# Chunked linear attention feeding a bilinear FFN: the inter-block products in 64x64 tiles of the array

## The chip, the core and the metric

The kernel runs on one core of a Trainium2 chip. The metric is device time in microseconds, the median over several executions. The core has a matrix engine (TensorE, "PE" in the profile, with its weight loads shown as "PEld"), a vector engine (VectorE, "DVE"), an activation engine (ScalarE, "ACT"), GpSimdE ("POOL"), and a queue of DMA issues on SyncE ("SP"). Matrix products are written to PSUM, a memory in banks. DVE and ACT carry results from PSUM to SBUF.

## What is computed

`q`, `k`, `v` are `[4, 8, 768, 64]` (batch, heads, sequence, head width), `lam` is one decay for each head. The reference walks over blocks of the sequence:

```python
intra = einsum('bhic,bhjc->bhij', qb, kb) * Dmask        # lam**(i-j) for i >= j, else 0
intra = einsum('bhij,bhjd->bhid', intra, vb)
inter = einsum('bhid,bhde->bhie', qb * lam_pow, kv_state) # what earlier blocks left
out   = intra + inter
kv_state = lam_block * kv_state + einsum('bhsd,bhse->bhde', kb_dec, vb)
...
x = out as [3072, 512]                                    # heads side by side
result = ((x @ w_a) * (x @ w_b)) @ w_out                  # w_a, w_b: 512x1536, w_out: 1536x512
```

## The kernel before

**Units.** The sequence is cut into blocks of 128 rows. A unit is one block of one batch with all 8 heads, so there are 4 x 6 = 24 units (`NB` = 6 for each batch), and unit `u` follows unit `u-1` in its batch unless `u % NB == 0`. The decay is folded into the operands: `make_qs` and `make_ks` multiply q by `lam**pos` and k by `lam**-pos` (POOL, L272 and L277), so that the state is a plain running sum, and the mask is plain lower-triangular.

**One unit's attention.** Its q and k are turned to `qT`, `kT` with heads in pairs: pair `hp` holds heads `2hp` and `2hp+1` in partitions 0-63 and 64-127. `scores` (L323) makes 8 products, K = 64 rows of the array each, the two heads of a pair in two PSUM banks. `masks` (L340, DVE) makes bf16 copies of both banks under the triangle. `intra` (L365) makes 8 products with `vb`, each 64 columns wide, into one PSUM bank `o_ps` `[128, 4, 128]`. `inter` (L355) adds 4 products of 128x128: the state of a pair is kept as a 128x128 matrix with the two heads' 64x64 states on its diagonal and zeros elsewhere. `evac_o` (L372) copies the bank to `xT`, the input of the FFN.

**The state.** `kv_mms` (L379) accumulates `k^T v` of a unit in the PSUM bank `kvd`, 4 products of 128x128 (whole pairs, so that the off-diagonal blocks hold products of different heads). `kv_copy` (L411, DVE) multiplies 128x512 of it by a mask `bdiag` of ones on the diagonal blocks, into `st_bufs`. Where a pair of units has just gone through `pieces_O`, `kv_beside` (L400) adds the second unit's state with 8 products of 64 columns instead.

**The FFN.** Units are taken in groups of `GROUPS = (4, 1, 2, 4, 4, 4, 4, 1)`. For a group, each of 12 column chunks `f` gives 4 products for `a_ps`, 4 for `b_ps` (both L449), an ACT copy to `a_sb` (L457) and a DVE product `ab` (L462); then 12 products for each unit make `op` (L482), ACT copies it (L477) and SP stores it.

**Order.** The schedule is manual: the program's order is each engine's order. `ffn` calls `hook(slot)` after each chunk, and the table `PLAN` says which attention pieces of later units are put there: `P` (load, scale and transposition by DMA), `V` (`kv_update` and `kv_copy`), `S` (`scores`, `masks`), `O`/`O2` (`pieces_O` for one or two units) and `Q` (`pieces_O` for two units, with the scores of the next two in between). PSUM banks are handed out in rotation, 7 of them, by `ps_bank`; the eighth holds `kvd`.

**Start.** The first four units go another way: q and k arrive packed (`x4`), are scaled by `scale4` on DVE (L553), transposed on PE (`transpose4`), scored (`scores4`), and their state and outputs are made before the FFN begins. All loads stand in one queue in the order q, k, v, then the weights in chunks of 512 KB (`w_a` chunk 0, 1, `w_b` chunk 0, 1, ...); `cast_w` turns each chunk to bf16. `cast_w("a", 0, "first")` (L171 to L173) splits the first chunk between DVE and POOL. In the first group chunk `f = 0` is made in two column cuts, units 0-2 and then unit 3.

Of the kernel before, what the change touches and what calls it, by code (L numbers as in the profile page):

```python
# [66 lines left out]
def kernel(  # L67
# [94 lines left out]
    def cast_w(kind, c, eng):  # L162
        t = staged.pop((kind, c))
        if kind == "o":
            dst = wo_sb[:, 2 * c:2 * c + 2, :]
        else:
            dst = w_part(wa_sb if kind == "a" else wb_sb, c)
        if eng == "act":
            nc.scalar.copy(dst, t)  # L169
        elif eng == "first":  # L170
            nc.vector.tensor_copy(dst[:, :2, :128], t[:, :2, :128])  # L171
            nc.gpsimd.tensor_copy(dst[:, 2:, :128], t[:, 2:, :128])
            nc.gpsimd.tensor_copy(dst[:, :, 128:], t[:, :, 128:])  # L173
        else:
            nc.vector.tensor_copy(dst, t)  # L175
        pump()
# [39 lines left out]
    for w, src in (("q", q), ("k", k)):  # L216
        x4_r = src[0, :, 0:PACK * BLK, :].rearrange("h (p r) d -> p h (r d)", r=PACK)
        n_h = 4 if w == "q" else 2
        for h in range(0, H, n_h):
            t = wst_pool.tile([128, 1024], F32, name=w + "4", tag="wst")[:, :n_h * 256]  # L220
            nc.sync.dma_start(out=t.rearrange("p (h x) -> p h x", h=n_h), in_=x4_r[:, h:h + n_h])
            t = t.rearrange("p (h r d) -> p h r d", h=n_h, r=PACK)
            for hh in range(0, n_h, 2):
                x4[w, h + hh] = t[:, hh:hh + 2]
            staged[w + "4", h] = t
# [20 lines left out]
    bdiag = singles.tile([128, 2, 64], BF16, name="bdiag")  # L246
    nc.gpsimd.memset(bdiag, 0.0)
    nc.gpsimd.memset(bdiag[0:64, 0, :], 1.0)
    nc.gpsimd.memset(bdiag[64:128, 1, :], 1.0)
    st_bufs = [singles.tile([128, HP, 2, D], BF16, name=f"st{i}") for i in range(4)]  # L250
    for t in st_bufs:
        nc.gpsimd.memset(t, 0.0)
# [8 lines left out]
    bdiag_bc = _bc(bdiag, [bdiag.ap[0], [0, HP], [1, 128]])  # L261
# [7 lines left out]

    def make_ks(u, eng):  # L270
        qk = prep_pool.tile([128, 2, H, D], BF16, name="qk", tag="qk")
        eng_of(eng).tensor_mul(qk[:, 1], raw.pop((u, "k")),  # L272
                               lp_k[:, u % NB].to_broadcast([128, H, D]))
        U[u] = dict(qk=qk, kn=qk[:, 1])

    def make_qs(u, eng):
        eng_of(eng).tensor_mul(U[u]["qk"][:, 0], raw.pop((u, "q")),  # L277
                               lp_q[:, u % NB].to_broadcast([128, H, D]))
# [65 lines left out]
    def o_bank(u):  # L344
        first = "o" not in U[u]
        if first:
            U[u]["o"] = ps_bank("o_ps", [128, HP, 128], F32)
        return first

    def inter(u):  # L350
        d = U[u]
        if u % NB > 0:
            first = o_bank(u)
            for hp in range(HP):
                nc.tensor.matmul(d["o"][:, hp, :], lhsT=st_bufs[(u - 1) % 4][:, hp, :, :],  # L355
                                 rhs=d["qT"][:, hp, :], start=(first and hp == 0), stop=True,
                                 skip_group_check=True)

    def intra(u, first=False):
        d = U[u]  # L360
        first = o_bank(u) or first
        for hp in range(HP):
            for i in range(2):
                p = slice(64 * i, 64 * i + 64)
                nc.tensor.matmul(d["o"][p, hp, :], lhsT=d["vb"][:, 2 * hp + i, :],  # L365
                                 rhs=d["m"](i, hp), start=(first and hp == 0),
                                 stop=True, skip_group_check=True)

    def evac_o(u, xT, col, eng="act"):
        o_ps = U[u].pop("o")  # L370
        if eng == "act":
            nc.scalar.copy(xT[:, :, col:col + BLK], o_ps)  # L372
        else:
            nc.vector.tensor_copy(xT[:, :, col:col + BLK], o_ps)

    def kv_mms(ps, w, hps, first):
        d = U[w]
        for hp in hps:
            nc.tensor.matmul(ps[:, hp, :, :], lhsT=d["kn"][:, 2 * hp:2 * hp + 2, :],  # L379
                             rhs=d["vb"][:, 2 * hp:2 * hp + 2, :], start=(first and hp == 0),  # L380
                             stop=True, skip_group_check=True)

    def kv_bank():
        kv["ps"] = kvps_pool.tile([128, HP, 2, D], F32, name="kvd", tag="kvd")
# [9 lines left out]
    def kv_beside(u):  # L394
        if u % NB == 0 or u % NB == NB - 1:
            kv_update(u)
        for hp in range(HP if 0 < u % NB < NB - 1 else 0):
            for i in range(2):
                p = slice(64 * i, 64 * i + 64)
                nc.tensor.matmul(kv["ps"][p, hp, i, :], lhsT=U[u]["kn"][:, 2 * hp + i, :],  # L400
                                 rhs=U[u]["vb"][:, 2 * hp + i, :],
                                 start=False, stop=True, skip_group_check=True)

    def kv_copy(u, ps, eng="dve"):
        st = st_bufs[u % 4]
        if eng == "act":
            for i in range(2):
                p = slice(64 * i, 64 * i + 64)
                nc.scalar.copy(st[p, :, i, :], ps[p, :, i, :])
        else:  # L410
            nc.vector.tensor_mul(st[:].rearrange("p hp i d -> p hp (i d)"),  # L411
                                 ps[:].rearrange("p hp i d -> p hp (i d)"), bdiag_bc)
# [11 lines left out]
    def pieces_O(us, nxt=()):  # L424
        kqs = [score_banks() for u in nxt]
        for u in us:
# [3 lines left out]
        for u in us:  # L430
            intra(u)
            xT, col = xTs[u]
            evac_o(u, xT, col)
        if len(us) == 2 and us[0] >= n0 + 5:
            kv_beside(us[1])
        for u, kq in zip(nxt, kqs):
            masks(u, kq)
        if len(us) == 2 and us[0] >= n0 + 5 and us[1] % NB < NB - 1:
# [6 lines left out]
    def half(w_sb, f, xT, gt, name, cuts=None):  # L445
        ps = ps_bank(name, [128, 512], F32, ffn=True)
        for lo, hi in cuts or ((0, gt),):
            for s in range(KS):
                nc.tensor.matmul(ps[:, lo:hi], lhsT=w_sb[:, s, f * 128:(f + 1) * 128],  # L449
                                 rhs=xT[:, s, lo:hi], start=(s == 0), stop=(s == KS - 1),  # L450
                                 skip_group_check=bool(cuts))
        return ps

    def a_part(f, xT, gt, cuts=None):
        ps = half(wa_sb, f, xT, gt, "a_ps", cuts)
# [3 lines left out]

    def b_part(f, xT, gt, a_sb, ab):  # L460
        ps = half(wb_sb, f, xT, gt, "b_ps")
# [23 lines left out]
    def ffn(u0, n, xT, hook, first, last):  # L485
        gt = n * BLK
        ab = ab_pool.tile([128, FC, 512], BF16, name="ab", tag="ab")
        if first:
            for i, cs in enumerate(W_STEPS):
                nxt = W_STEPS[i + 1] if i + 1 < len(W_STEPS) else ()  # L490
                fs = range(w_off[cs[0]] // 128, w_off[cs[-1] + 1] // 128)
                a_sbs = [a_part(f, xT, gt, ((0, gt - BLK), (gt - BLK, gt)) if f == 0 else None)
                         for f in fs]
# [57 lines left out]
    def scale4(w, i, j):  # L551
        hs = slice(4 * i + 2 * j, 4 * i + 2 * j + 2)
        nc.vector.tensor_mul(  # L553
            xs4[w].rearrange("p r (h d) -> p h r d", d=D)[:, hs],
            x4[w, hs.start],
            (lp_q if w == "q" else lp_k)[:, NB:, hs, :].rearrange("p r h o -> p h r o")
            .to_broadcast([128, 2, PACK, D]))
        if w == "k" or j == 1:
            staged.pop((w + "4", 4 * i + (2 * j if w == "k" else 0)))
# [173 lines left out]
```

## Time and profile before

| | |
|---|---|
| median of 5 runs | 232.93 us (232.57 to 233.85) |
| the profiled execution's own time | 232.71 us |
| its span in the profile | 231.0 us, so 1.71 us lie around it |
| PE busy | 225.1 us (97%), 1763 products |
| DVE, ACT, POOL busy | 117.1, 88.7, 50.8 us |
| granted TensorE clock | 1.0 |
| DMA | 39.36 MB, mean 170 GB/s |

A line of the timeline has its start and its length in us, the engine, the line of the kernel, the operation, output and inputs, shapes, how many instructions were merged, and in brackets the idle time before it with what ended it. The length of a merged row of products includes the way of the last one through the array; so the time that a group of products takes from PE is read as the start of the next group less its own start. `128*64` in a PE row says how many rows and columns of the array each product uses; the shape after it is rows by streamed columns.

### The profile page before, as it was taken

How to read it: one execution, taken by the hardware profiler on the slowest of the kernel's cores; microseconds unless marked ns; L12 is line 12 of the kernel's file. 1: busy time of each engine (PE TensorE's matmuls, PEld its weight loads, DVE VectorE, ACT ScalarE, POOL GpSimd, SP SyncE). 2: the span in 40 equal slices, each digit the busy share in tenths (PEclk: the TensorE clock that was granted, in tenths of full speed). 3: DMA queues.
4: the chain of work that ended last, by engine and by line, in shares of the span. 5: the costliest groups of instructions: out<-in, count | busy, mean ns of one | idle time of the engine just before them, and what ended most of it. 6: DMA issues, size and time to landing. Idle time of an engine off the chain costs nothing.

```text
span 231.0 us, 4496 instructions
## 1 busy us (share of the span) xinstructions
PE 225.1 (97%) x1763; PEld 124.1 (54%) x1763; DVE 117.1 (51%) x205; ACT 88.7 (38%) x170; POOL 50.8 (22%) x65
## 2 busy tenths in 40 slices
PE   7899999999999999999999999999999999999994
PEld 2575444459687554554544454544454544444493
DVE  0894856636569738675324583325583313332050
ACT  3577553066442243342233342233332234332261
POOL 6061000238351444433301533002100000000000
PEclk9999999999999999999999999999999999999999
DMA  4999999999999999999969996239200220000311
GB/s 149 305 279 350 364 386 270 306 218 193 207 207 175 219 193 210 224 184 232 356 207 204 215 186 100 91 115 207 45 3 0 91 91 3 1 0 18 121 45 48
DMA packets 97509, 39.36 MB, mean 170 GB/s; under 512 B 85456, under 2 KB 91984, under 8 KB 97488
## 3 DMA queue, kind: packets, MB, share of 16 engines
q1 hardware_dynamic: 97200, 39.00, 74.4%
q8 instruction: 14, 0.23, 0.4%
q10 hardware_dynamic: 288, 0.07, 0.1%
q14 instruction: 7, 0.06, 0.1%
HBM read 28.32 MB, written 6.29 MB: 150 GB/s over the span
## 4 chain that ended last, share of the span: by engine, by line
PE 91%; DMA 3%; DVE 3%; ACT 1%; issue 1%; SPq 0%; DVEq 0%
PE a_ps L449 27%; PE op L482 27%; PE b_ps L449 26%; PE o_ps L365 3%; DMA q<-in_q_dram 3%; PE kq L323 2%; PE o_ps L355 2%; PE kvd L379 1%; ACT scratch L576 1%; DVE m L340 1%; DVE ab L462 1%; PE tps L309 1%; DVE scratch L553 1%; PE kq L601 1%; DVE st L411 0%
## 5 line engine op out<-in xcount | busy, mean ns | idle before, releaser
L462 DVE TENSOR_TENSOR ab<-a_sb,b_ps 128x512 bf16<-128x512 bf16 (+2 forms) x96 | 52.2, 552 | 76.7 <-PE b_ps L449 57.8
L449 PE MATMUL a_ps<-xT,wa_sb 128*128 128x512 bf16 (+3 forms) x388 | 76.9, 324 | 0.2 <-ACT xT L372 0.2
L449 PE MATMUL b_ps<-xT,wb_sb 128*128 128x512 bf16 (+2 forms) x384 | 76.9, 326 | 0.0
L457 ACT CAST a_sb<-a_ps 128x512 bf16<-128x512 f32 (+2 forms) x96 | 45.2, 480 | 62.3 <-PE a_ps L449 62.2
L482 PE MATMUL op<-wo_sb,ab 128*128 128x512 bf16 (+2 forms) x312 | 65.6, 363 | 0.0
L449 PEld LDWEIGHTS <-wb_sb 128*128 128x128 bf16 x384 | 34.5, 98 | 28.6 <-ACT wb_sb L169 0.2
L449 PEld LDWEIGHTS <-wa_sb 128*128 128x128 bf16 x388 | 34.0, 98 | 28.6 <-DVE wa_sb L175 0.8
L482 PEld LDWEIGHTS <-ab 128*128 128x128 bf16 x312 | 28.7, 98 | 30.0
L340 DVE TENSOR_TENSOR m<-kq,lotri 128x512 bf16<-128x512 f32 x47 | 29.3, 683 | 18.3 <-PE kq L323 17.7
L272 POOL TENSOR_TENSOR qk<-kf,lp_k 128x512 bf16<-128x512 f32 x18 | 19.0, 1053 | 73.7 <-DMA kf<-in_k_dram 58.4
L277 POOL TENSOR_TENSOR qk<-qf,lp_q 128x512 bf16<-128x512 f32 x20 | 22.0, 1101 | 22.5 <-DMA qf<-in_q_dram 22.5
L477 ACT COPY o_sb<-op 128x512 f32<-128x512 f32 (+2 forms) x19 | 10.3, 540 | 34.0 <-PE op L482 34.0
L372 ACT CAST xT<-o_ps 128x512 bf16<-128x512 f32 x22 | 12.0, 588 | 18.5 <-PE o_ps L365 17.9
L411 DVE TENSOR_TENSOR st<-kvd,bdiag 128x512 bf16<-128x512 f32 x18 | 12.3, 683 | 3.4 <-PE kvd L379 3.4
L286 DVE CAST vb<-vf 128x512 bf16<-128x512 f32 x17 | 10.8, 636 | 1.7 <-DMA vf<-in_v_dram 1.3
L208 PE MATMUL idle<-idle_sb 128*128 128x128 bf16 (+1 forms) x31 | 7.7, 392 | 1.3 <-DVE idle_sb L203 1.3
L365 PE MATMUL o_ps<-m,vb 128*64 128x128 bf16 x192 | 7.8, 222 | 0.0
L286 POOL CAST vb<-vf 128x512 bf16<-128x512 f32 x7 | 4.8, 679 | 13.8 <-DMA vf<-in_v_dram 13.8
L355 PEld LDWEIGHTS <-st 128*128 128x128 bf16 x80 | 5.4, 98 | 3.2 <-issue 0.4
L311 ACT COPY qkT<-tps 128x1024 bf16<-128x1024 bf16 x3 | 3.0, 1012 | 10.4 <-PE tps L309 10.4
L323 PE MATMUL kq<-qkT 64*128 64x128 bf16 x160 | 6.7, 218 | 0.0
L169 ACT CAST wb_sb<-wst 128x1024 bf16<-128x1024 f32 x5 | 5.2, 1046 | 3.3 <-DMA wst<-in_moe_w_b_dram 3.3
(58 smaller groups left out, 85.7 us busy)
## 6 DMA issues: line engine op xcount, KB each, us to landing
vf<-in_v_dram SPq DMA_DIRECT2D x24, 256.0 KB, 4.9
qf<-in_q_dram SPq DMA_DIRECT2D x20, 256.0 KB, 4.3
kf<-in_k_dram SPq DMA_DIRECT2D x20, 256.0 KB, 4.8
out_dram<-o_sb SPq DMA_DIRECT2D x16, 256.0 KB, 2.0
wst<-in_moe_w_a_dram SPq DMA_DIRECT2D x6, 512.0 KB, 8.6
wst<-in_moe_w_b_dram SPq DMA_DIRECT2D x6, 512.0 KB, 9.1
wst<-in_moe_w_out_dram SPq DMA_DIRECT2D x6, 512.0 KB, 10.7
out_dram<-o_kept SPq DMA_DIRECT2D x7, 256.0 KB, 3.4
```

The costliest lines, as they stand in the source:

```text
L272: eng_of(eng).tensor_mul(qk[:, 1], raw.pop((u, "k")), lp_k[:, u % NB].to_broadcast([128, H, D]))
L277: eng_of(eng).tensor_mul(U[u]["qk"][:, 0], raw.pop((u, "q")), lp_q[:, u % NB].to_broadcast([128, H, D]))
L286: eng_of(eng).tensor_copy(vb, vf)
L323: nc.tensor.matmul(kq[i][:, hp, :], lhsT=d["kT"][p, hp, :], rhs=d["qT"][p, hp, :], start=True, stop=True, skip_group_check=True)
L340: nc.vector.tensor_mul(m, kq[i], lotri_bc)
L365: nc.tensor.matmul(d["o"][p, hp, :], lhsT=d["vb"][:, 2 * hp + i, :], rhs=d["m"](i, hp), start=(first and hp == 0), stop=True, skip_group_c ...
L372: nc.scalar.copy(xT[:, :, col:col + BLK], o_ps)
L411: nc.vector.tensor_mul(st[:].rearrange("p hp i d -> p hp (i d)"), ps[:].rearrange("p hp i d -> p hp (i d)"), bdiag_bc)
L449: nc.tensor.matmul(ps[:, lo:hi], lhsT=w_sb[:, s, f * 128:(f + 1) * 128], rhs=xT[:, s, lo:hi], start=(s == 0), stop=(s == KS - 1), skip_gro ...
L457: nc.scalar.copy(a_sb[:, :gt], ps[:, :gt])
L462: nc.vector.tensor_mul(ab[:, f, :gt], a_sb[:, :gt], ps[:, :gt])
L482: nc.tensor.matmul(op[:, lo:hi], lhsT=ab[:, f, t * 128:(t + 1) * 128], rhs=wo_sb[:, f, lo:hi], start=(f == 0), stop=(f == FC - 1))
```

## The change

1. Heads are paired 4 apart: pair `c` holds heads `c` and `c+4`. `scale` writes q and k in that order with a pattern of four dimensions, and the packed loads of the start bring heads `c` and `c+4` (4 loads of q instead of 2, of half the size).
2. `inter` makes 8 products of 64 rows and 64 columns of the array for a unit, in the order of the four quarters, instead of 4 of 128x128.
3. `kv_mms` makes 8 products of 64 columns (streaming 64) for every update instead of 4 of 128x128; `kv_beside` goes. The state is kept without zero blocks: `kv_copy` is a plain copy of 128x256, `bdiag` and the clearing of `st_bufs` go.
4. A pair of units shares two `o_ps` banks, one for heads 0-3 and one for heads 4-7 (the row halves of the array that write them), and `evac_o` copies a bank for both units at once. A single unit takes two banks and two smaller copies.
5. At the start, the first two chunks `f` are made in two column halves (units 0, 1, then 2, 3: `a_parts`), DVE casts three quarters of the first weight columns instead of a half, and intra and inter products of units 0 to 3 stand in a new order.

The core of the diff:

```diff
-            nc.vector.tensor_copy(dst[:, :2, :128], t[:, :2, :128])
-            nc.gpsimd.tensor_copy(dst[:, 2:, :128], t[:, 2:, :128])
+            nc.vector.tensor_copy(dst[:, :3, :128], t[:, :3, :128])
+            nc.gpsimd.tensor_copy(dst[:, 3:, :128], t[:, 3:, :128])
...
-        n_h = 4 if w == "q" else 2
-        for h in range(0, H, n_h):
-            t = wst_pool.tile([128, 1024], F32, name=w + "4", tag="wst")[:, :n_h * 256]
-            nc.sync.dma_start(out=t.rearrange("p (h x) -> p h x", h=n_h), in_=x4_r[:, h:h + n_h])
...
+        x4_r = x4_r.rearrange("p (b c) x -> p c b x", b=2)
+        n_c = 2 if w == "q" else 1
+        for c in range(0, HP, n_c):
+            t = wst_pool.tile([128, 1024], F32, name=w + "4", tag="wst")[:, :n_c * 512]
+            t = t.rearrange("p (c b x) -> p c b x", c=n_c, b=2)
+            for cc in range(n_c):
+                nc.sync.dma_start(out=t[:, cc], in_=x4_r[:, c + cc])
...
-    st_bufs = [singles.tile([128, HP, 2, D], BF16, name=f"st{i}") for i in range(4)]
-    for t in st_bufs:
-        nc.gpsimd.memset(t, 0.0)
+    st_bufs = [singles.tile([128, HP, D], BF16, name=f"st{i}") for i in range(4)]
...
+    def scale(eng, dst, x, lp):
+        eng_of(eng).tensor_mul(dst.rearrange("p (c b) d -> p b c d", b=2),
+                               x[:].rearrange("p (b c) d -> p b c d", b=2),
+                               lp.rearrange("p (b c) o -> p b c o", b=2)
+                               .to_broadcast([128, 2, HP, D]))
...
+    def o_banks(us, ats=(None, None)):
+        for b, at in enumerate(ats):
+            ps = ps_bank("o_ps", [128, 2, 2, BLK], F32, at=at)
+            for n, u in enumerate(us):
+                U[u].setdefault("o", []).append(ps[:, :, n, :])
...
+    def o_mm(u, b, c, **ops):
+        h = 4 * b + c
+        p = slice(64 * (h % 2), 64 * (h % 2) + 64)
+        new = U[u]["flags"]
+        nc.tensor.matmul(U[u]["o"][b][p, c // 2, :], start=new[b, h % 2], stop=True,
+                         skip_group_check=True, **ops)
...
     def inter(u):
...
-                nc.tensor.matmul(d["o"][:, hp, :], lhsT=st_bufs[(u - 1) % 4][:, hp, :, :],
-                                 rhs=d["qT"][:, hp, :], start=(first and hp == 0), stop=True,
-                                 skip_group_check=True)
+            for c in range(HP):
+                for b in range(2):
+                    p = slice(64 * b, 64 * b + 64)
+                    o_mm(u, b, c, lhsT=st[p, c, :], rhs=U[u]["qT"][p, c, :])
...
+    def intra(u, b):
+        for c in range(HP):
+            o_mm(u, b, c, lhsT=U[u]["vb"][:, 4 * b + c, :], rhs=U[u]["m"](b, c))
...
+    def kv_mms(ps, w, cs, first):
+        d = U[w]
+        for c in cs:
+            for b in range(2):
+                nc.tensor.matmul(ps[64 * b:64 * b + 64, c, :], lhsT=d["kn"][:, 2 * c + b, :],
+                                 rhs=d["vb"][:, 4 * b + c, :], start=(first and c == 0),
                                  stop=True, skip_group_check=True)
...
-            nc.vector.tensor_mul(st[:].rearrange("p hp i d -> p hp (i d)"),
-                                 ps[:].rearrange("p hp i d -> p hp (i d)"), bdiag_bc)
+            nc.vector.tensor_copy(st, ps)
...
+        for b in range(2):
+            for u in us:
+                intra(u, b)
+            evac_o(us, b)
...
+    def a_parts(fs, xT, gt):
+        ps_parts[0] = True
+        pss = [half(wa_sb, f, xT, "a_ps", 0, gt // 2) for f in fs]
+        a_sbs = []
+        for f, ps in zip(fs, pss):
+            half(wa_sb, f, xT, "a_ps", gt // 2, gt, ps)
+            a_sbs.append(a_copy(ps, gt))
```

## Prediction

> **What bounds the kernel now.** I read the busy time by stage first, then PE's own timeline, then what PE waited for. By stage:
>
> ```profile
> core 0: us, PE busy (x) PEld busy (x) DVE busy (x) ACT busy (x) POOL busy (x), PEclk, DMA share, GB/s
> 5.00:20.00 15.00, 13.94 (x184) 9.36 (x183) 12.27 (x20) 10.06 (x20) 4.63 (x7) 1.00 1.14 307
> 20.00:60.00 40.00, 40.00 (x310) 22.12 (x308) 24.51 (x46) 19.29 (x36) 9.12 (x10) 1.00 1.08 290
> 60.00:220.00 160.00, 159.69 (x1141) 83.86 (x1140) 76.45 (x126) 53.51 (x98) 33.36 (x32) 1.00 0.69 138
> ```
>
> From 20 us on PE has no idle time worth naming and the granted clock is 1.0. So a product that goes is time that goes, and work saved on DVE, ACT or POOL counts only where PE waits for it. PE's timeline over one stretch gives every price that I need; "cost" is the next row's start less the row's own:
>
> ```profile
> 75.22 0.39 PE L355 MATMUL o_ps<-qkT,st 128*128 128x128 bf16 x4
> 75.87 0.38 PE L355 MATMUL o_ps<-qkT,st 128*128 128x128 bf16 x4 [0.27 <-DVE ab L462]
> 76.19 0.62 PE L323 MATMUL kq<-qkT 64*128 64x128 bf16 x16
> 76.74 0.64 PE L365 MATMUL o_ps<-m,vb 128*64 128x128 bf16 x16
> 77.31 1.47 PE L482 MATMUL op<-wo_sb,ab 128*128 128x512 bf16 x6
> 78.61 0.39 PE L379 MATMUL kvd<-vb,qk 128*128 128x128 bf16 x4
> 78.84 1.46 PE L482 MATMUL op<-wo_sb,ab 128*128 128x512 bf16 x6
> 80.13 0.61 PE L355 MATMUL o_ps<-qkT,st 128*128 128x128 bf16 x8
> 80.67 0.64 PE L365 MATMUL o_ps<-m,vb 128*64 128x128 bf16 x16
> 81.14 0.29 PE L400 MATMUL kvd<-vb,qk 128*64 128x64 bf16 x8
> 81.36 1.47 PE L482 MATMUL op<-wo_sb,ab 128*128 128x512 bf16 x6
> ```
>
> - A full product streaming 128 columns: 4 of L379 between two L482 cost 0.23 us, 56 ns each by the single starts in the trace.
> - Products on halves of the array go in pairs: 16 of L365 cost 0.47 us (80.67 to 81.14), 56 to 59 ns a pair; the partners start 3 to 4 ns apart. Pairs streaming 64 columns (L400) follow after 25 to 32 ns.
> - **Changing the shape in which the array is used costs extra.** The same 16 of L365 cost 0.57 us when full products follow (76.74 to 77.31) and 0.47 us when L400, of the same shape, follows. Eight of L355 cost 0.54 us (80.13 to 80.67) instead of 8 x 56 ns = 0.45 us. By the single starts every change of shape, to or from 64 rows or 64 columns, adds 93 to 99 ns: I take 0.095 us.
>
> **Inter, a unit.** Before: 4 x 56 = 224 ns, full shape. After: 8 products of 64x64 in the order of the four quarters, two groups of four. No row has this shape. Lower bound: four side by side in the 56 ns that a pair takes now, 112 ns a unit. Upper bound: only two side by side, 224 ns. I take the lower, since the trace shows two row halves side by side (L323) and two column halves side by side (L365), each with its own weight loads, and L400 starts 8 products in 95 ns, so eight starts in 112 ns are no new pace. In return the shape changes once more: in each place where inter stands, it came straight after full products and now needs a change. For a single unit: +95 - 112 = -17 ns. For two units: +95 - 224 = -129 ns. PE's built order has, from 20 us on, 5 places with one unit and 6 with two: -0.085 - 0.774 = **-0.86 us**. If only pairs run side by side, it is 11 x 95 ns = +1.05 us.
>
> The Trainium skill has two rules against this change. "TensorEngine Tiling (Array Packing)", Key Properties, says that a change of tiling mode drains the engine; it gives no price, and the 93 to 99 ns above are one. "TensorE: Matmul & The Clock Gate", Part 1, says that start-to-start never drops below about 25 ns, however small the product; by that rule eight products would take 200 ns and the inter term would be 17 x 88 ns = 1.5 us worse. The trace has partners 3 to 4 ns apart, so here the measurement decides.
>
> **State updates.** Before: 4 full products, 224 ns. After: 8 of 64 columns as L400. Where the update stands alone among full products (10 places from 20 us on), it costs 95 ns to get in, 95 ns from first to last start, 128 ns to the next full product: 318 ns, +94 ns each, **+0.94 us**. Where it comes right after intra (2 places) the shape is already there: before 152 + 168 + 56 = 376 ns, after 53 + 95 + 128 = 276 ns, **-0.20 us**. Where L400 stood already, nothing changes. Over the whole program the built order has 80 changes of shape instead of 47; 31 of the 33 new ones are in these sums, two at the start.
>
> Sum of PE's own stream: -0.86 + 0.94 - 0.20 = **-0.12 us**. What the four quarters save is nearly spent on getting in and out of them.
>
> **PE's stalls.** There are three from 20 us on, and DVE makes two of them. The largest is above, 0.43 us before 75.87, and DVE had been busy without a gap since 69.33:
>
> ```profile
> 69.33 1.24 DVE L286 CAST vb<-vf 128x512 bf16<-128x512 f32 x1 [0.40 <-POOL qk L272]
> ...
> 70.83 0.68 DVE L411 TENSOR_TENSOR st<-kvd,bdiag 128x512 bf16<-128x512 f32 x1
> 71.43 0.74 DVE L462 TENSOR_TENSOR ab<-a_sb,b_ps 128x256 bf16<-128x256 bf16 x2
> 72.09 2.47 DVE L340 TENSOR_TENSOR m<-kq,lotri 128x512 bf16<-128x512 f32 x4
> 74.48 0.40 DVE L462 TENSOR_TENSOR ab<-a_sb,b_ps 128x256 bf16<-128x256 bf16 x1
> 74.81 0.68 DVE L411 TENSOR_TENSOR st<-kvd,bdiag 128x512 bf16<-128x512 f32 x1
> 75.41 0.40 DVE L462 TENSOR_TENSOR ab<-a_sb,b_ps 128x256 bf16<-128x256 bf16 x1
> ```
>
> L411 occupies DVE for 0.60 us (74.81 to 75.41). A copy of 128x256 from PSUM should be like L462 at 128x256, 0.33 us (74.48 to 74.81); between 0.33 and 0.60 I take 0.33. Two of them in this chain give 0.54 us back. Inter's second bank is freed by the last `ab`, now at about 75.3, and PE comes there at about 75.45 (0.135 us of added cost by then, and the new change of shape): the stall goes, **-0.43 us**. A second one, 0.10 us before `a_ps` at 25.32, waits for a weight cast queued behind L411 (23.38): with the shorter copy and PE 0.09 us later it goes, **-0.10 us**. The third, 0.20 us inside the scores at 71.36, waits for a DMA transposition that lands at 71.57. That does not move, but PE arrives about 0.24 us later through its added state updates, so these eat it: **-0.20 us**. If POOL's scaling with four dimensions were slower (1.04 us now; DVE does the same pattern in 688 ns against 680 flat), this landing is the place that would show it; elsewhere transpositions land two microseconds ahead.
>
> **Start.** Everything before 20 us can gain at most a few hundredths, by the weights:
>
> ```profile
> 17.20 0.52 POOL L172 CAST wa_sb<-wst 128x256 bf16<-128x256 f32 x1 [0.81 <-DMA wst<-in_moe_w_a_dram]
> 18.03 3.68 PE L449 MATMUL a_ps<-xT,wa_sb 128*128 128x384 bf16 x20 [0.23 <-ACT xT L372]
> 19.06 0.69 DVE L175 CAST wa_sb<-wst 128x1024 bf16<-128x1024 f32 x1 [0.75 <-DMA wst<-in_moe_w_a_dram]
> ```
>
> The DMA queue moves about 350 GB/s (less for v's small pieces) without a break from 4 us, and the bytes ahead of the weights are unchanged. The first chunk lands at 17.15, the second at 19.03, its cast ends at 19.75, and chunk `f = 2` starts at 19.81, where PE already waits 50 ns. The changed kernel can start `f = 0` at about 17.6 instead of 18.03, since units 0 and 1 are evacuated first, DVE and POOL finish the first columns together, and 16 products of 256 columns cost 16 x 109 = 1.75 us as before. PE then waits at 19.5 for the same cast: **0**, with 0.3 us of cover. Beyond that cover, lateness of `xT` or of the casts costs one for one. The two more DMA issues (about 0.5 us of SP each) come before issues that wait for queue space until 7.5 us; shorter state copies on ACT, cleared memsets on POOL and earlier scaling on DVE all end in front of the same landing.
>
> **Evacuations.** Pairs: two copies of 128x512 as before. Single units: two of 128x256 on ACT (372 ns each) instead of one of 588 ns, behind at least 0.8 us of `op` products: 0; uncovered it would be 0.1 us, twice. More banks at once: the rotation gives inter banks whose readers ended 0.2 us earlier or more, except the `ab` case above.
>
> **Sum.** -0.12 - 0.43 - 0.10 - 0.20 = -0.85 us. Against the profiled execution, 232.71 - 0.85 = 231.86; the median of the runs stands 0.22 us above that execution, so I give **232.1 us**. Half a per cent, 1.16 us, is about what a measurement of this kernel can tell from no change; the forecast is inside it, 0.33 us from its edge.
>
> **Rivals.**
> - *The waits come back elsewhere* (the copy stays near 0.60 us, or the freed bank is another's): only PE's own -0.12 remains, 232.8 us. For: DVE stays busy in that stretch. Against: nothing else in the chain grows.
> - *The start moves after all*: the smaller first loads let the queue run earlier and the second weight chunk lands sooner, by up to the 0.43 us that `f = 0` can gain: 231.6 us. Against: the queue is full from 4 us and the bytes are the same.
> - *The four quarters run only two at a time*, slower than before: inter +1.05 instead of -0.86, sum +1.06, so 234.0 us; with the stalls kept, +1.79, so 234.7 us. It decides when a group of four costs more than 81 ns: there are 34 groups, and 34 x 25 ns is the 0.85 us. For: no row shows 64x64. Against: rows and columns are each shown side by side.
>
> **How the numbers follow.** The forecast has 0.60 (own range 231.5 to 232.7), returning waits 0.12, the earlier start 0.13, two at a time 0.15. The range 231.1 to 234.0 reaches over the earlier start and the first form of the slow case, and leaves its second form and sums of lucky ends out. Faster than 231.77: a quarter of the forecast (0.15) and nearly all of the earlier start, 0.27. Slower than 234.09: most of two at a time with some stalls kept, 0.12. The rest, 0.61, within half a per cent.
>
> **What would show it.** Right: inter of one unit spans about 0.11 us and its starts come in fours; lone `kvd` rows cost 0.32 us; no PE idle near 75; L411's successor near 0.33 us between starts; `f = 2` still at about 19.8 behind a cast that waits for the DMA. Wrong: fours farther apart than 81 ns, a change into 64x64 dearer than 0.1 us, scores waiting longer for `qkT`, or a weight landing that moved.

## The result, and the profile after

| | before | after |
|---|---|---|
| median | 232.94 us (232.25 to 235.71, 46 runs) | 234.96 us (233.8 to 236.16, 27 runs) |
| profiled execution | 232.71 us | 234.68 us |
| its span | 231.0 us | 233.0 us |
| PE products | 1763 | 1919 |
| granted clock | 1.0 | 1.0 |

The ratio is 1.0069, 95% interval 1.0051 to 1.0087: the changed kernel is slower, by more than the prediction's bound of half a per cent, and its median lies outside the range. The medians themselves, each over all runs, stand 2.0 us apart. The page of after, part 1 (busy time) and the row of part 3 for the queue that carries instructions; the same row of before has 14 packets and 0.23 MB:

```profile
PE 224.0 (96%) x1919; PEld 120.1 (52%) x1919; DVE 113.0 (49%) x205; ACT 88.1 (38%) x170; POOL 47.7 (20%) x58
q8 instruction: 15, 0.25, 0.5%
```

DVE has 4.1 us less to do, as meant, and PE is not busier than before (225.1 us); yet the span grew by 2.0 us. The timeline of PE in after, over the stretch that the prediction showed of before:

```profile
76.57 0.42 PE L359 MATMUL o_ps<-qkT,st 64*64 64x128 bf16 x16
76.92 0.62 PE L325 MATMUL kq<-qkT 64*128 64x128 bf16 x16
77.47 0.64 PE L359 MATMUL o_ps<-m,vb 128*64 128x128 bf16 x16
78.04 1.47 PE L496 MATMUL op<-wo_sb,ab 128*128 128x512 bf16 x6
79.44 0.32 PE L390 MATMUL kvd<-vb,qk 128*64 128x64 bf16 x8
79.69 1.47 PE L496 MATMUL op<-wo_sb,ab 128*128 128x512 bf16 x6
```

The first row is inter: 16 products on quarters, and no idle time in front of it, where before had 0.27 us in brackets and 0.43 us of stall in all. `kvd` alone among full products costs 0.25 us from its first start to the next row, and it is entered late (79.44, behind an `op` row of six that now costs 1.40 us instead of 1.30).

Lateness along the run shows where the time went. Each number is the start of a `kvd` row less that of its counterpart in before, whose own time heads the column. (Narrow rows include 0.1 us for the change of shape ahead of them; the last four kernels are experiments told below.)

| kernel | 22.4 | 51.5 | 69.1 | 81.1 | 98.6 | 183.7 |
|---|---|---|---|---|---|---|
| after | +1.01 | +1.04 | +1.31 | +0.77 | +1.80 | +1.83 |
| after_again | +1.07 | +1.10 | +1.36 | +0.82 | +1.69 | +1.72 |
| after_lean | +0.23 | +0.26 | +0.53 | -0.02 | -0.11 | -0.06 |
| lean_pe48 | +0.54 | +0.57 | +0.83 | +0.29 | +1.43 | +1.46 |
| wide_all | +0.82 | +0.82 | +0.83 | +0.67 | +1.89 | +1.51 |
| wide_mix | +0.54 | +0.55 | +0.78 | +0.24 | +0.43 | +0.04 |

The stream that the prediction priced, from 22.4 us on, is a little faster, as forecast. Two steps spoil it: about a microsecond before 22.4, and another between 81.1 and 98.6.

**The first step.** The timeline of after at the start:

```profile
18.36 0.42 DVE L171 CAST wa_sb<-wst 128x384 bf16<-128x384 f32 x1 [1.52 <-DMA wst<-in_moe_w_a_dram]
...
18.84 3.35 PE L449 MATMUL a_ps<-xT,wa_sb 128*128 128x256 bf16 x22 [1.12 <-DVE wa_sb L171]
...
19.85 0.69 DVE L175 CAST wa_sb<-wst 128x1024 bf16<-128x1024 f32 x1 [0.47 <-DMA wst<-in_moe_w_a_dram]
```

The first weight chunk lands at 18.34 us instead of 17.15, the second at 19.83 instead of 19.03; PE begins the FFN at 18.84 instead of 18.03, and `f = 2` starts at 20.74 instead of 19.81: +0.93 us. The view of the DMA engines from 4 to 20 us shows why the weights are late. Its first row is their mean busy share in 40 slices of 0.4 us, its last what they moved. Before:

```profile
DMA  9999999999999999999999999999999999999999
DMA packets 8124, 4.98 MB, mean 311 GB/s; under 512 B 4305, under 2 KB 8123, under 8 KB 8123
```

And after:

```profile
DMA  8999999999999999999999799669999999999999
DMA packets 7959, 4.77 MB, mean 298 GB/s; under 512 B 4336, under 2 KB 7958, under 8 KB 7958
```

Before has no slice below nine tenths. After has a hole at 12.8 to 14.8 us, while v's small pieces are loaded, and has moved 0.21 MB less by 20 us: at the 350 GB/s at which weights come, 0.6 us of the 0.8 to 1.2 us by which these chunks are late.

**The second step.** The timeline of PE in after, near 98 us:

```profile
98.24 0.40 PE L325 MATMUL kq<-qkT 64*128 64x128 bf16 x8
99.58 0.40 PE L325 MATMUL kq<-qkT 64*128 64x128 bf16 x8 [0.95 <-DMA qkT<-qk]
```

In before the scores of the two units stood together:

```profile
97.46 0.62 PE L323 MATMUL kq<-qkT 64*128 64x128 bf16 x16
```

Now the second eight start 1.34 us after the first eight, for want of unit 14's transposition. Followed back in the chain of waits, this is a line of transfers that began at 84.3 us, each step behind the one before it: SP's issue of unit 12's transposition, load of a later k (87.1 to 92.6), scaling on POOL, transposition of unit 14. The DMA view of after from 83 to 90 us (slices of 0.175 us):

```profile
DMA  9545998999999989999999999690000000599999
q8 instruction: 1, 0.02, 1.0%
qkT<-qk SPq DMA_TRANSPOSE x2, 5.2
```

And of before, in the same stretch:

```profile
DMA  9998335469999999990099966999899999999999
qkT<-qk SPq DMA_TRANSPOSE x2, 4.4
```

In after one packet of instructions (16 KB) falls into this stretch, at 86.8 us, and from 87.6 to 88.9 the DMA engines stand nearly idle (1 to 18 GB/s against 200 to 300 around it), with unit 12's transposition open, which lands 5.9 us after its issue, and that load of k. Before has no such packet between 81.5 and 100.1 us, and only short dips. The trace has one packet of this queue for about every 256 PE instructions (a product and its weight load are two): 3526 of them and 14 packets before, 3838 and 15 after. The change adds 312 PE instructions, 72 of them ahead of the FFN, so every later packet comes at another moment.

### The profile page after: what moved, and what is told of

Its sections match the earlier page's. It is cut to its first block, busy times and chain, and to the rows that moved or that the text cites. A ratio compares the mean times of both kernels' runs of the same rounds, so it can differ in the third digit from the quotient of the medians.

```text
span 233.0 us, 4801 instructions
## 1 busy us (share of the span) xinstructions
PE 224.0 (96%) x1919; PEld 120.1 (52%) x1919; DVE 113.0 (49%) x205; ACT 88.1 (38%) x170; POOL 47.7 (20%) x58
## 4 chain that ended last, share of the span: by engine, by line
PE 83%; DMA 9%; SPq 4%; POOL 2%; issue 0%; DVE 0%; ACT 0%; POOLq 0%
PE op L496 27%; PE a_ps L449 25%; PE b_ps L449 24%; PE o_ps L359 4%; DMA wst<-in_moe_w_a_dram 3%; SPq L130 3%; DMA kf<-in_k_dram 2%; PE kq L325 2%; DMA q<-in_q_dram 2%; POOL qk L269 2%; DMA qkT<-qk 2%; PE kvd L390 1%; SPq L297 1%; PE tps L311 1%; SPq L224 0%
## 5 line engine op out<-in xcount | busy, mean ns | idle before, releaser
L449 PE MATMUL a_ps<-xT,wa_sb 128*128 128x512 bf16 (+2 forms) x392 | 77.1, 323 | 1.1 <-DVE wa_sb L171 1.1
L382 ACT CAST xT<-o_ps 128x512 bf16<-128x512 f32 (+1 forms) x24 | 12.1, 555 | 19.7 <-PE o_ps L359 19.7
L411 DVE CAST st<-kvd 128x256 bf16<-128x256 f32 x18 | 7.5, 416 | 2.9 <-PE kvd L390 2.9
L208 PE MATMUL idle<-idle_sb 128*128 128x128 bf16 (+1 forms) x31 | 6.6, 347 | 1.3 <-DVE idle_sb L203 1.3
L288 POOL CAST vb<-vf 128x512 bf16<-128x512 f32 x7 | 4.3, 610 | 16.8 <-DMA vf<-in_v_dram 16.8
L359 PEld LDWEIGHTS <-vb 128*64 128x64 bf16 x192 | 5.8, 109 | 1.4 <-POOL vb L288 0.2
```

What stands on the lines that cost most here:

```text
L288: eng_of(eng).tensor_copy(vb, vf)
L359: nc.tensor.matmul(U[u]["o"][b][p, c // 2, :], start=new[b, h % 2], stop=True, skip_group_check=True, **ops)
L382: nc.scalar.copy(dst, src)
L411: nc.vector.tensor_copy(st, ps)
```

## The experiments

**Both kernels once more** (`before_again`, `after_again`).

> The kernel of before once more, for a second profile of its start and of its load queue. If the changed start is the change's doing, the second weight chunk lands again near 19.0 us and chunk f = 2 starts near 19.8 us; if it was chance, they move by several tenths of a us here too.

> The changed kernel once more. If both losses are its own, the second weight chunk lands near 20.1 us, f = 2 starts near 21.0 us, and PE waits again about 1.1 us inside the scores near 98.7 us for a DMA transposition. If chance, one of the two is gone or moved by more than half.

232.61 us and a span of 230.9 for before, 234.59 and 232.9 for after. The two steps come back (row of the table above), the first in another form: the first two weight chunks land at 17.0 and 18.6, but PE stands still for 1.12 us after eight products of the FFN with nothing in the profile that it waits for (timeline of PE), and the first `w_b` chunk lands at 21.05 (20.54 before). Near 98 us PE waits 0.79 us.

```profile
17.75 1.04 PE L449 MATMUL a_ps<-xT,wa_sb 128*128 128x256 bf16 x8
19.91 1.26 PE L449 MATMUL a_ps<-xT,wa_sb 128*128 128x256 bf16 x9 [1.12 <-issue]
```

In this second execution of each kernel the loss is nearly the same size; its place is not fixed. The stop itself is at a fixed place. It stands ahead of the same product, the ninth of the FFN, in four traces of the changed program: after_again, after_look3 (0.80 us), after_q2 (0.62) and after_kvfull (0.19). In all four an instruction packet runs shortly before (17.63 to 18.60 us here), and PE goes on 1.3 to 1.5 us after the packet's end. In after the packet ended at 16.1 us and there is no such stop. That PE waits for its instructions is therefore likely; no experiment isolates it.

**Splitting q's loads alone** (`before_q4`): before, with each of the two packed loads of q issued in two halves.

```diff
-            nc.sync.dma_start(out=t.rearrange("p (h x) -> p h x", h=n_h), in_=x4_r[:, h:h + n_h])
+            for h2 in range(0, n_h, 2):
+                nc.sync.dma_start(out=t.rearrange("p (h x) -> p h x", h=n_h)[:, h2:h2 + 2],
+                                  in_=x4_r[:, h + h2:h + h2 + 2])
```

> Before, with each of the two packed q loads of the start (512 KB) given out as two of 256 KB; nothing else. Theory A (two more loads ahead of the weights delay the queue): the second weight chunk lands about 1.1 us later than before, near 20.1 us, f = 2 starts near 21 us, and the time rises by 0.8 to 1.2 us, ratio 1.0035 to 1.005. Rival (the late start comes from the new order of products, casts and copies): weights land as before, 19.0 us, ratio 1.000 within 0.001.

233.64 against 232.84 us, ratio 1.0028 (1.0010 to 1.0046). In its profile `b` starts at 22.57 instead of 21.55, behind this cast, since its chunk landed at 21.79 instead of 20.54 (timeline):

```profile
21.82 0.69 DVE L175 CAST wb_sb<-wst 128x1024 bf16<-128x1024 f32 x1 [1.99 <-DMA wst<-in_moe_w_b_dram]
...
22.57 1.04 PE L451 MATMUL b_ps<-xT,wb_sb 128*128 128x512 bf16 x4 [0.78 <-DVE wb_sb L175]
```

By 20 us the DMA engines had moved 4.83 MB instead of 4.98. So the split alone, with no other part of the change, makes the start 1.02 us late, 0.4 of which was given back by the stall near 75 us. The place is not the one expected: the first weight chunk landed 0.5 us late, the second at 19.11 (19.03 before), and only the third made PE wait. An instruction packet runs from 18.17 to 19.22 here, from 15.5 to 16.6 in before. In the ten profiles whose first packet starts at 16.5 us or later, one of the first weight chunks lands 2.1 to 2.7 us after the chunk ahead of it; in the other five the largest step is 1.9 us, the common one 1.5. So the bytes that are missing and the moment of the packet may both enter, and this run does not part them.

**A longer lookahead for the loads** (`after_look3`): the theory that unit 14's loads are issued too late.

```diff
-            elif c >= used["u"] + LOOKAHEAD.get(used["u"], 2 if used["u"] > 8 else 3):
+            elif c >= used["u"] + LOOKAHEAD.get(used["u"], 2 if used["u"] > 15 else 3):
```

> The changed kernel, with loads given out three units ahead instead of two for units 9 to 15. Theory B (from unit 9 on load, scaling, transposition and the next load form a loop whose latency PE has caught up with): the 1.1 us wait inside the scores near 98.7 us goes and the ratio to before falls from 1.007 to about 1.002 (0.9 to 1.1 us less). Rival (the DMA engines themselves are too busy there): more loads ahead bring nothing, the wait stays above 0.8 us, or moves to the next unit, ratio 1.006 to 1.008.

238.2 us, 1.0224 (1.0198 to 1.0251). The theory fell. PE waits 1.16 us at 91.8 and 1.96 us at 101.7, the second time for a transposition issued at 97.15 us (unit 14's was issued at 95.13 in after); that it stood behind the further loads is a reading, not a test. And then this (busy time by stage; PEclk is the granted clock):

```profile
core 0: us, PE busy (x) PEld busy (x) DVE busy (x) ACT busy (x) POOL busy (x), PEclk, DMA share, GB/s
100.00:103.00 3.00, 1.27 (x28) 1.17 (x30) 2.04 (x5) 0.26 (x1) 1.95 (x2) 0.84 1.21 227
103.00:106.00 3.00, 3.00 (x20) 1.26 (x15) 0.81 (x2) 1.40 (x3) 1.49 (x2) 0.59 1.38 159
```

After 1.7 idle microseconds in the first window the granted clock is 0.59 in the next three, so here the wait costs more than its own length.

**PE instructions alone** (`before_pe72`): before, with 72 more PE instructions in the warm-up that fills the time until the first data come, for the same number of streamed columns.

```diff
-    warm(13, 512)
+    warm(49, 136)
```

> Before, with the 13 warm-up products of 512 columns at the start made as 49 of 136 columns: the same columns and time on PE, 72 more PE instructions (36 products, 36 weight loads), as many as the change adds ahead of the FFN. Theory C (PE's instructions arrive in pieces of 256 through the busy DMA engines; more of them ahead of the FFN means that a refill hits the weights or leaves PE without instructions, and later refills hit the loads of units 9 to 14): f = 2 starts 0.6 to 1.2 us later or PE waits on issue near 20 us, and the scores near 97.5 us wait 0.3 us or more; ratio 1.003 to 1.009. Rival (instructions cost only PE time, which here is hidden): ratio 1.000 within 0.001.

233.01 against 232.51 us, 1.0016 (1.0002 to 1.0030). The start is no later in its DMA view (4.99 MB by 20 us); the `kvd` row of 22.4 us is 0.22 us late. The scores near 98 us, however, wait for unit 14's transposition (timeline of PE):

```profile
98.08 0.40 PE L323 MATMUL kq<-qkT 64*128 64x128 bf16 x8 [0.31 <-DMA qkT<-qk]
```

Its instruction packet comes at 94.9 us, inside that transposition (92.3 to 98.0). Between 81.1 and 98.6 us its rows fall back by 0.48 us. So instructions that do nothing can go with a wait at this place, and here they did not bring the late start of after. A wait of 0.31 us is weak evidence, though: before_warm24 below has one of 0.20 us there with no packet between 83.5 and 101.2 us.

**Fewer PE instructions ahead of the FFN** (`after_lean`): after, with 48 taken out: the states of units 0 and 1 by full products, and short warm-up products merged.

```diff
-        warm(4)
+        warm(1, 512)
...
-            kv_mms(sts[u], w, hps, w == 0)
+            if u == 2:
+                kv_mms(sts[u], w, hps, w == 0)
+                continue
+            for c in hps:
+                nc.tensor.matmul(sts[u][:, c, :, :], lhsT=U[w]["kn"][:, 2 * c:2 * c + 2, :],
+                                 rhs=U[w]["vb"][:, c::4, :], start=(w == 0 and c == 0),
+                                 stop=True, skip_group_check=True)
```

> The changed kernel with 48 fewer PE instructions ahead of the FFN: the states of units 0 and 1 made by full products and copied in two halves, and runs of short warm-up products of 128 columns made as one wide product. Theory C: no wait on issue near 18.6 us, f = 2 starts at 20.2 us or earlier instead of 20.9 to 21.0, the time falls by 0.5 to 1.2 us, ratio 1.002 to 1.005. Rival (only the weights' landing counts): f = 2 near 20.9 us, ratio 1.006 to 1.008.

233.1 against 232.51 us, 1.0021 (1.0011 to 1.0031), where after has 1.0069. The first step is nearly gone (4.94 MB by 20 us), and the second wholly; the scores stand together again (timeline of PE):

```profile
97.45 0.62 PE L325 MATMUL kq<-qkT 64*128 64x128 bf16 x16
```

Yet a packet falls into the line of transfers here too, at 90.9 us, and the transposition then open takes 5.8 us. It is unit 13's, the engines do not stop behind the packet, and unit 14's lands in time. So a packet in the line is not enough to make PE wait.

**The same number put back** (`lean_pe48`): after_lean with 48 harmless instructions in the warm-up.

```diff
-    warm(13, 512)
+    warm(37, 180)
```

> The variant with 48 fewer PE instructions ahead of the FFN, with those 48 put back in the warm-up of the first 6 us: 37 products of 180 columns instead of 13 of 512, the same time on PE. Theory C (the number of PE instructions ahead of the FFN decides, whatever they are): PE waits on issue for about 1 us between 18 and 20 us, or a weight chunk lands about 1 us later, f = 2 starts at 20.5 us or later, the scores near 98 us wait 0.4 us or more; ratio 1.005 to 1.008. Rival (the full products for the first states, or the wide warm-up products, made the gain by themselves): as without the 48, f = 2 near 19.5 us, ratio 1.001 to 1.003.

235.0 against 232.94 us, 1.0091 (1.0058 to 1.0124). A later start is back in part (+0.54 at 22.4 against +0.23; 4.64 MB by 20 us), and the wait near 98 us wholly:

```profile
99.21 0.40 PE L325 MATMUL kq<-qkT 64*128 64x128 bf16 x8 [1.06 <-DMA qkT<-qk]
```

The packet comes at 86.1 us, as in after, and the engines stand nearly idle from 87.3 to 88.6. The two kernels differ in nothing but warm-up products.

**Fewer warm-up instructions in before** (`before_warm24`): the same merging, 24 instructions less.

> Before, with its 18 short warm-up products made as 6 wide ones: 24 fewer PE instructions. Theory C: refills come a little later than before; the one of 69.4 us moves to about 71, the one of 100 us stays outside the tight stretch; ratio 0.998 to 1.001. Rival (wide warm-up products are themselves what helped): ratio below 0.998.

233.08 against 232.94 us, 1.0014 (0.9994 to 1.0035): no difference that this measurement can tell. The packets moved about as expected (70.6 and 101.2 us).

**Two loads of q in after** (`after_q2`): heads 0 to 3 and 4 to 7, scaled in these halves.

```diff
+        if w == "q":
+            for b in range(2):
+                t = wst_pool.tile([128, 1024], F32, name="q4", tag="wst")
+                t = t.rearrange("p (h x) -> p h x", h=4)
+                nc.sync.dma_start(out=t, in_=x4_r[:, 4 * b:4 * b + 4])
```

> The changed kernel with q's packed loads as two of 512 KB again (heads 0 to 3, heads 4 to 7), and q scaled in the same halves; nothing else. Theory A with C: the loads behind them are issued about 0.5 us sooner and the first weight chunks land about 0.6 us sooner, the time falls by 0.3 to 0.8 us, ratio 1.0035 to 1.0055. Rival (PE's missing instructions alone set the start): f = 2 stays at 20.9 us, ratio 1.006 to 1.008.

234.8 against 232.51 us, 1.0120 (1.0083 to 1.0157). The hole among the loads is gone (4.97 MB by 20 us, first chunks at 16.6 and 18.0 us), but a transposition of a pair now needs both halves of q, the attention of the first units ends later (PE waits 2.23 us for scaled operands at 8.1 us), the stop at the ninth product takes 0.62 us, and the `kvd` row of 22.4 us is 1.71 us late. Here the hole is gone together with the four loads. But after_lean, after_kvfull and after_look3 have four loads and no slice below nine tenths between 5 and 20 us, so four loads alone do not always make it.

**Full products for lone states, with narrow copies** (`after_kvfull`): 4 products of 128x128 where the update stands alone, and the diagonal blocks copied in two halves.

```diff
-        else:
-            nc.vector.tensor_copy(st, ps)
+        for b in range(2):
+            p = slice(64 * b, 64 * b + 64)
...
+                nc.vector.tensor_copy(st[p], ps[p, :, b, :])
```

> The changed kernel with the ten lone state updates as 4 full products each (the off-diagonal blocks are made and not read) and the state copied in two halves of 64 partitions; 80 fewer PE instructions from 20 us on. By the prices read in the trace after: a lone update costs 224 instead of 340 ns, 10 x 0.117 = 1.2 us less on PE; the longer copy brings back up to 0.3 us of wait near 75 us; 0.9 to 1.2 us less, ratio 1.002 to 1.004, and further 0.5 us less if a refill of PE instructions leaves the stretch of 65 to 97 us. Rival (PE's extra time is covered by the waits at 20 and 98 us): ratio 1.006 to 1.008.

233.74 against 232.51 us, 1.0066 (1.0052 to 1.0080). The updates cost 223 ns again, but (groups by line)

```profile
L417 DVE CAST st<-kvd 64x256 bf16<-64x256 f32 x36 | 15.0, 417 | 3.7 <-PE kvd L390 3.1
```

a copy of 64 partitions takes 417 ns, as long as one of 128 partitions in after (416 ns). Two of them occupy DVE for longer than the masked copy of before, and PE stands still for 0.64 us near 77 us and 0.39 us near 26. Its instruction packet comes at 91.4 us, in the line of transfers, with unit 13's transposition open for 5.9 us; unit 14's lands at 98.87 us instead of 99.54 in after, and the scores near 98 us take only 0.2 us longer than in before.

**One half copied on ACT** (`best1`): after_lean, full lone updates, one half of the copy on each engine.

```diff
-            nc.vector.tensor_copy(st, ps)
+            nc.vector.tensor_copy(st[:64], ps[:64, :, 0, :])
+            nc.scalar.copy(st[64:], ps[64:, :, 1, :])
```

> The variant with 48 fewer PE instructions at the start, and besides the ten lone state updates as 4 full products each, the state copied half on DVE and half on ACT. A lone update then costs 224 instead of 340 ns: 1.2 us less on PE than that variant (ratio 1.002 to before); the DVE half copy takes 0.44 us of DVE instead of 0.33 us, up to 0.2 us of wait near 75 us: ratio 0.9965 to 0.999, faster than both kernels. Rival (another wait takes its place, as with both halves on DVE): ratio 1.001 to 1.004.

234.83 against 232.94 us, 1.0076 (1.0046 to 1.0105). The ACT half stands ahead of `a_sb` and waits for DVE (timeline):

```profile
72.33 0.37 ACT L418 CAST st<-kvd 64x256 bf16<-64x256 f32 x1 [2.43 <-DVE st L417]
```

Through these 2.43 us, `a_sb` and `ab` come late and PE stands still for 1.03 us near 73 and 1.2 us near 78.

**The state in whole pairs again, inter in quarters** (`wide_all`; `wide_mix` keeps the narrow state for units 6 to 11): after_lean, `kvd` of 128x512 copied plainly, since inter reads the diagonal blocks alone.

```diff
-            nc.vector.tensor_copy(st, ps)
+        elif eng == "dve" and WIDE(u):
+            nc.vector.tensor_copy(st[:].rearrange("p c b d -> p c (b d)"),
+                                  ps[:].rearrange("p c b d -> p c (b d)"))
```

> The changed kernel with the 48 instructions of after_lean taken out, and the state kept again as whole pairs (128x512 in PSUM): lone updates and those of unit 2 are 4 (12) full products, DVE copies 128x512 plainly, and only inter stays in four 64x64 quarters. PE has 360 instructions ahead of the first FFN product, as before (361). If a lone update's price (340 against 224 ns, measured in the traces) is PE's own loss, ten of them give 1.17 us back against after_lean; the wide copy brings DVE's two stalls back (up to 0.53 us), so 232.4 us, between 231.9 and 232.9. If the loss lies with the 64x64 products themselves, it stays at or above after_lean, 233.1 us. If PE's instruction transfers are what moves the start, f = 2 begins at or before 19.8 us.

> As wide_all, but the second batch (units 6 to 11, where DVE makes PE wait near 75 us) keeps the change's narrow state: 8 products of 64 columns and a copy of 128x256. Of the ten lone updates four stay narrow (+0.47 us against wide_all) and the stalls near 75 us (0.43 us) and 71 us (0.20 us) go again. Expected: within 0.2 us of wide_all, 232.2 us; PE's own sum against the kernel before is then -0.20 + 0.06 - 0.60 + 4 x 0.117 = -0.27 us and the stalls -0.63 us. If the stalls come back whatever the width of the copy, it is slower than wide_all by 0.5 us.

234.23 and 233.57 against 232.92 us: 1.0047 (1.0024 to 1.0070) and 1.0036 (1.0008 to 1.0064). Both missed their numbers, though PE's stream did what was expected: from 22.4 to 183.7 us wide_mix gains 0.50 us on before, and wide_all 0.35 us besides its wait of 1.04 us near 98. That wait is the second step once more (DMA view of wide_all, 93 to 100 us):

```profile
DMA  9999999999999999999999900000006999999999
q8 instruction: 1, 0.02, 1.2%
qkT<-qk SPq DMA_TRANSPOSE x2, 5.7
```

An instruction packet comes in unit 14's transposition, the engines stand idle for 1.2 us behind it, and the transposition takes 5.8 us. Its number of PE instructions ahead of the FFN is that of before (360 against 361), so this number does not by itself decide where later packets fall. And both start late (4.74 and 4.86 MB by 20 us), against what the expectation allowed: the hole in the loads does not follow PE's instruction count. In wide_all `f = 2` starts at 19.84, near what was expected, and the loss comes with the first `w_b` chunk, at 21.58, behind a packet of 18.0 to 19.2 us.

No version was faster than before.

## Why the prediction was wrong

**PE's own stream: right in kind, three of four terms off in size.** By the single starts in the trace of after:

| term | predicted | measured |
|---|---|---|
| lone update, 10 places | 318 - 224 = +94 ns | 93 + 119 + 128 = 340, +117 ns |
| update after intra, 2 places | -100 ns | -100 ns |
| inter of one unit, 5 places | -17 ns | 93 + 90 + 146 = 329 against 316, +13 ns |
| inter of two units, 6 places | -129 ns | 443 against 543, -100 ns |
| sum | -0.12 us | 1.17 - 0.20 + 0.06 - 0.60 = +0.43 us |

The bet on four quarters held: eight products start within 90 ns and fours follow each other after 56 ns, so the rival "two at a time" is out. Partners in quarters start 3 to 4 ns apart, like those of halves. The term that was mis-sized is the change of shape, 0.095 us: it counts the delay up to the first start and leaves out that the second step of the new shape is longer too. In after the second four of inter starts 80 ns after the first, the later fours 56 ns apart; the second pair of a lone update starts 52 ns after the first instead of 28. The trace of before already had it: in the row at 80.67 us (L365) the second pair starts 80 ns after the first, the later ones 56, and an average of 56 to 59 ns a pair hides this. 24 ns in 10 lone updates and 11 places of inter make 0.50 us of the 0.55 us between the two sums. The Trainium skill's floor of about 25 ns from start to start ("TensorE: Matmul & The Clock Gate", Part 1) does not hold for partners on quarters here, which start 3 to 4 ns apart. Its statement that a change of tiling mode drains the engine ("TensorEngine Tiling (Array Packing)", Key Properties) agrees with the 93 to 103 ns by which every change of shape put off the next start here too.

**The stalls: right.** All three went (0.43, 0.10 and 0.20 us), with the copy at 0.33 us between starts as taken. So PE's stream as a whole is +0.43 - 0.73 = -0.30 us, against -0.85 predicted. after_lean, where neither step occurs, confirms it: from +0.23 at 22.4 us to -0.06 at 183.7, a gain of 0.29 us.

**The start: wrong.** The step that failed is "**0**, with 0.3 us of cover". It rested on the bytes ahead of the weights, which did not change, and on the issues, which come early enough. It did not ask whether the engines stay as well filled when q comes in four loads instead of two. They do not: before_q4 shows the late start with the split alone, and over all profiles the five with two loads had moved 4.97 to 4.99 MB by 20 us, the ten with four loads 4.64 to 4.94 MB. It also put the 72 further PE instructions ahead of the FFN at nothing; in four traces of the changed program PE stops at its ninth FFN product, 1.3 to 1.5 us from the end of an instruction packet. The late start cost 0.93 us in the profiled execution, there by late weights.

**The transpositions: wrong.** The failed sentence is "elsewhere transpositions land two microseconds ahead". In before, that of unit 14 lands at 97.49 us and its products start at about 97.7: 0.2 us ahead. The prediction looked at the landing where a wait stood already and not at those with the least slack. It also took the DMA queue for one with loads, transpositions and stores in it; the instructions that PE fetches were in the page (part 3) and were not counted, although the change adds 312 of them. It cost 1.11 us. The prediction's last paragraph did name "scores waiting longer for `qkT`" and "a weight landing that moved" as signs of being wrong; its sum had no price for either.

**The sum.** -0.30 + 0.93 + 1.11 = +1.74 us; the last group of products starts 1.84 us later and the span is 2.0 us longer, so 0.26 us of it is not assigned. None of the rivals named this: "the start moves" was weighed as a gain alone.

**What is shown and what is not.** Shown: the split of q by itself delays the start; 48 idle PE instructions by themselves bring a wait of a microsecond near 98 us and a longer time (1.0091 against 1.0021). Leaving the longer lookahead aside, in each profile with 0.3 us or more of this wait an instruction packet falls into the line of transfers from unit 12 to unit 14 (after, after_again, lean_pe48, before_pe72, wide_all), and the DMA engines idle behind it. The reverse does not hold: after_lean, after_kvfull, wide_mix and after_q2 have a packet in that line too, and wait 0.28 us or less. Where in the line it falls, and how late PE comes, seem to decide. Argued only: that the packet itself makes the idle time, and that PE's stop at the ninth FFN product is want of instructions. Open: how the late start divides between missing bytes and the moment of the packet; and what sets the size of the hole at the start among kernels with four loads, from after_lean's 4.94 MB to lean_pe48's 4.64; PE's instruction count does not order them, since wide_all and best1 have no more instructions there than after_lean and moved 4.74 and 4.69 MB. Two loads of q in pairs 4 apart, which would take the split out of the change, were not tried.

## What to carry to other kernels

Count the instructions that a change adds, not only their time: here they come over the DMA engines as one 16 KB packet for some 256 PE instructions, and where transfers are chained with little slack one packet can cost about a microsecond. For every landing that a forecast calls "hidden", read the slack of the tightest one in the trace, not that of the one which already waits. And a smaller DMA with the same bytes is not the same load: check that the engines stay busy in the view by slices.

## What the runs showed of the hardware

- Instructions share the DMA engines: behind such a packet the engines moved 0 to 18 GB/s for about 1.2 us, against 200 to 300 around it (after, wide_all); the transposition open at the time, between 82 and 98 us, took 5.4 to 6.2 us in nine traces (4.9 in after_again) instead of the 4.1 to 4.6 of before; and the load that SP issued then took 1.9 to 2.0 us to issue instead of 0.6 (after, wide_all, before_pe72).
- Products on quarters of the array run four at a time (fours 56 ns apart, 80 ns from the first to the second after a change of shape); partners on quarters start 3 to 4 ns apart, as those on halves do (after, before).
- A PSUM copy of 64x256 on DVE costs the same as one of 128x256 (417 and 416 ns), one of 128x512 with the mask 683 ns: columns cost, partitions did not (after_kvfull, after, before).
- After 1.7 us without products the granted clock was 0.59 over the next three microseconds (after_look3); after one idle microsecond of three (after, lean_pe48) it stayed at 1.0.
